# The end of an attention block on Trainium2: last logits on VectorE, last x on ScalarE, and the order of the work around them

## The chip, the cores and the metric

The kernel runs on one core of one Trainium2 chip. The metric is the time of one execution in microseconds (us), taken on the device. The core has five engines that run beside each other and meet at semaphores: TensorE (PE in the profile; PEld is its weight load), VectorE (DVE), ScalarE (ACT), GpSimd (POOL) and SyncE (SP), which here only issues DMA transfers. GpSimd issues DMAs too, among them the gathers and scatters by index.

## The reference

An attention block without softmax is followed by a mixture of experts with one expert per token:

```python
kv  = einsum('bhsd,bhse->bhde', k, v)            # batch 8, 8 heads, 576 tokens, head size 64
out = einsum('bhsd,bhde->bhse', q, kv)
out = out / sqrt(mean(out * out, -1) + 1e-6) * g_norm
x   = out.transpose(0, 2, 1, 3).reshape(4608, 512)

do     = x @ w_skip > 0                          # other tokens leave as they are
logits = x[do] @ w_gate                          # 8 experts
e      = argmax(logits);  p = softmax(logits)[e]
y      = relu(x[do] @ w1[e]) @ w2[e]             # 512 -> 1024 -> 512
result[do] = x[do] + p * y
```

All data are fp32.

## The kernel before

**Attention.** The kernel works through 36 units, `n` = 0 to 35; two neighbouring units (`u` = 0 and 1, four heads each) make 256 tokens' x. In step `n` of the main loop several units are in flight at once: `turn(n+1)` transposes q, `root(n-1)` (L525, ScalarE) takes the square root of the mean of squares, `values(n)` multiplies q with the state (L496, or L504 for units 34 and 35, which hold the ninth token of each group of nine) into a PSUM tile and squares it on ScalarE (L510), `squares(n)` sums the squares on VectorE (L518), and `norm(n-1)` takes the reciprocal (L532) and multiplies the PSUM tile by it (L537, `xl`). The state's columns hold, beside the 64 values of a head, 9 columns at each end with which the logits of the gate and the skip score come out of the same product. So an `xl` has both x and the parts of the logits. `finish(n-1)` adds the parts up on GpSimd (L554 for each unit, L558 and L562 for each pair, into `lg`), and puts the product of x with g_norm (L567, GpSimd, 128x512) on the list `late`. `scale` empties this list: for a unit it is called in the next unit's `norm`, where it waits for the reciprocal; the products of units 33 to 35 are emptied at step 36 behind the last instruction of the choice (L634). After a pair's second product, its x is stored to DRAM, by SP (L602, L591) or by GpSimd (L598).

PSUM tiles set part of the order: `o_ps` has two buffers, and units 30 and 33 use `sum_ps` in their place. A unit's L496 or L504 can start when the `xl` of the unit two before it (three for unit 33: unit 30) has read the tile.

**Queues.** The order of the instructions on each engine is that of the program, written by hand: `at(step, part, job)` puts a job into one of the parts of a step ("early", before `values`; "mid", after it; "pe", after `norm`; "dve"; "end"). No planner moves them.

**The choice and the slots.** Tiles of 128 tokens are gated in three groups, of 12, 10 and 14 tiles. `choose` (L614 to L634, VectorE) finds each token's expert, `rank` (L645 to L651, TensorE) counts places with triangular and full matrices of ones, `number` (L662 to L677, VectorE) splits each place into a column and a one-hot row (`oha_k`), `hits` (L690) and `weighed` (L698) make the columns, and `settle` (matmuls L710, sums L773) puts the token's row number into its slot. `NE` = 22 tiles are known before the last group. From the known ones `early` places the first 192 rows of the most frequent expert (`put`, L869 to L873, then `gather` L859 to L863, and `put_more`, L879, for the last 64 of them), `first_in` (L801, copies L828 and L830) turns these rows, and `first_layer_1` (L814, ReLU L817) starts the expert's first layer with them.

**The experts.** For the first expert `layer_1` (matmuls L1112, ReLU L1114 on ScalarE) and `layer_2` (L1124) work on the first 192 rows, f being the block of 128 of the 1024 hidden columns. Between these, TensorE takes up the rank and the slots of the last group, `again_rows` (L1051) copies indices of partial pieces between partitions, GpSimd gathers the remaining rows (L1084), and `expert_in` (L1093) turns them. Later experts follow one after another, with sums in the place of some products (L1192); each result is scattered by GpSimd (L1339). PSUM banks of the experts are the memory that the attention's tiles had: the third bank taken is the one of `first_layer_1`.

## Time and profile before

| | |
|---|---|
| median of 3 runs | 380.12 us (378.6 to 380.73) |
| the profiled execution | 381.81 us |
| its span | 380.0 us |
| TensorE busy in the span | 365.3 us (96%) |
| VectorE, ScalarE, GpSimd busy | 245.1, 142.3, 124.2 us |
| granted TensorE clock | 0.999 of full |

A span is the time from the first to the last instruction of one profiled execution. In a line of the timeline stand the start (us), the time of the whole run of equal instructions (us), engine, line of the program, operation, output and inputs, shapes and count; in brackets the idle time of the engine just before, and what ended it. A matrix product of fp32 shows as two records.

### The profile page before, as it was taken

To read this page: it belongs to the slowest core of one execution; us is meant where nothing else is said; L and a number is where in the kernel's file an instruction comes from. 1 tells how busy PE (TensorE), PEld (TensorE's weight loads), DVE (VectorE), ACT (ScalarE), POOL (GpSimd) and SP (SyncE) were. 2 spreads that over 40 slices of the span, in tenths; PEclk is the share of its full clock that TensorE was granted. 3 is DMA by queue.
4 is the path that set the end of the run, shared out by engine and by line. 5 is a ranking of instruction groups with operands and counts; after the bars stand their busy time and mean duration, and the time that the engine had idled before them with its cause. 6 is when DMAs were issued, how large, how long until landed. Compare 5 with 4: busy or idle time off the path is not lost.

```text
span 380.0 us, 9623 instructions
## 1 busy us (share of the span) xinstructions
PE 365.3 (96%) x3848; PEld 313.2 (82%) x3848; DVE 245.1 (64%) x626; ACT 142.3 (37%) x383; POOL 124.2 (33%) x195
## 2 busy tenths in 40 slices
PE   8999999999988998999999999999999999999994
PEld 4688797898977857779869987988988998998983
DVE  3344458667787961666756665875876876877831
ACT  2366676676774301214402430430440430431410
POOL 7025467655668544223013302212201211202003
PEclk9999999999999999999999999999999999999999
DMA  8999999996487738966516462672662762800001
GB/s 292 393 390 389 403 402 398 403 352 205 136 296 207 216 92 281 394 203 237 194 62 201 144 223 57 232 257 68 239 213 87 261 194 92 273 3 28 29 1 52
DMA packets 32039, 81.70 MB, mean 215 GB/s; under 512 B 2474, under 2 KB 2482, under 8 KB 31988
## 3 DMA queue, kind: packets, MB, share of 16 engines
q1 hardware_dynamic: 28176, 69.47, 52.1%
q0 software_dynamic: 3792, 11.53, 8.9%
q8 instruction: 32, 0.52, 0.6%
q14 instruction: 19, 0.16, 0.1%
q10 hardware_dynamic: 20, 0.02, 0.0%
HBM read 66.80 MB, written 14.48 MB: 214 GB/s over the span
## 4 chain that ended last, share of the span: by engine, by line
PE 84%; issue 6%; DVE 3%; ACT 3%; POOL 2%; DMA 1%; POOLq 0%; DVEq 0%; ACTq 0%
PE bank L1192 44%; PE bank L1124 9%; PE o_ps L496 6%; PE sum_ps L379 5%; PE bank L1112 4%; PE q_ps L460 3%; PE g_ps L393 2%; PE q_ps L170 2%; PE bank L1093 2%; DMA xg<-out_dram,src 1%; DVE rs L518 1%; DVE xl L537 1%; ACT sq L510 1%; PE q_ps L814 1%; PE g_ps L411 1%
## 5 line engine op out<-in xcount | busy, mean ns | idle before, releaser
L1202 ACT COPY p<-bank 128x128 f32<-128x128 f32 (+6 forms) x70 | 20.8, 297 | 100.3 <-PE bank L1192 89.3
L1192 PE MATMUL bank<-xt,w 128*128 128x128 f32 (+5 forms) x336 | 55.5, 288 | 0.1
L567 POOL TENSOR_TENSOR xb<-xl,g_b 128x512 f32<-128x512 f32 x36 | 44.4, 1234 | 32.5 <-DVE rs L532 30.6
L1192 PEld LDWEIGHTS bank<-xt,w 128*128 128x128 f32 x336 | 47.0, 190 | 2.0 <-DVE bank L1196 1.5
L1196 DVE TENSOR_TENSOR bank<-bank,p 128x128 f32<-128x128 f32 (+6 forms) x70 | 23.6, 337 | 37.1 <-PE bank L1192 36.0
L1192 PE MATMUL bank<-xs,s 128*128 128x128 f32 (+5 forms) x224 | 36.7, 289 | 0.0
L496 PE MATMUL o_ps<-kvd,qT 128*128 128x146 f32 x240 | 35.8, 290 | 1.0 <-ACT kvd L415 0.7
L1339 POOL DMA_INDIRECT out_dram<-xg,arows x9 | 10.0, 1112 | 78.7 <-DVE xg L1336 77.8
L518 DVE TENSOR_REDUCE rs<-sq 128x8 f32<-128x512 f32 x36 | 24.6, 682 | 16.2 <-ACT sq L510 16.0
L1124 PE MATMUL bank<-w,ht 128*32 128x128 f32 (+2 forms) x436 | 34.5, 319 | 0.0
L496 PEld LDWEIGHTS o_ps<-kvd,qT 128*128 128x128 f32 x240 | 31.6, 188 | 2.0 <-ACT kvd L415 1.5
L1192 PEld LDWEIGHTS bank<-xs,s 128*128 128x128 f32 x224 | 31.1, 190 | 1.0 <-ACT p L1202 0.8
L1339 POOL DMA_INDIRECT out_dram<-xg,rows x14 | 13.9, 994 | 53.2 <-DVE xg L1336 42.7
L1124 PEld LDWEIGHTS bank<-w,ht 128*32 128x32 f32 (+2 forms) x436 | 18.8, 120 | 13.2 <-issue 10.9
L537 DVE TENSOR_TENSOR xl<-o_ps,rs 128x584 f32<-128x584 f32 x34 | 26.1, 767 | 4.5 <-DVE rs L532 0.5
L1192 PE MATMUL bank<-t,ht 128*128 128x256 f32 x112 | 27.1, 385 | 0.0
L1192 PE MATMUL bank<-w,ht 128*128 128x256 f32 x112 | 27.1, 384 | 0.0
L1084 POOL DMA_INDIRECT xg<-out_dram,src x14 | 14.4, 1026 | 37.2 <-DMA out_dram<-xg,rows 13.9
L379 PE MATMUL sum_ps<-v,k 64*64 64x64 f32 x1152 | 25.6, 228 | 0.6 <-issue 0.6
L510 ACT ACTIVATE sq<-o_ps 128x512 f32<-128x512 f32 x34 | 20.3, 596 | 15.0 <-PE o_ps L496 14.5
L379 PEld LDWEIGHTS sum_ps<-v,k 64*64 64x64 f32 x1152 | 21.7, 140 | 4.7 <-issue 2.1
L1192 PE MATMUL bank<-t,hs 128*128 128x256 f32 x112 | 25.3, 379 | 0.0
(217 smaller groups left out, 680.5 us busy)
## 6 DMA issues: line engine op xcount, KB each, us to landing
w<-in_moe_w_dram SPq DMA_DIRECT2D x16, 2048.0 KB, 7.9
k<-in_k_dram SPq DMA_DIRECT2D x16, 576.0 KB, 9.7
v<-in_v_dram SPq DMA_DIRECT2D x16, 576.0 KB, 12.0
q<-in_q_dram SPq DMA_DIRECT2D x16, 576.0 KB, 9.2
out_dram<-xb SPq DMA_DIRECT2D x29, 256.0 KB, 4.4
out_dram<-xb POOLq DMA_DIRECT2D x7, 256.0 KB, 5.5
xg<-out_dram,src POOLq DMA_INDIRECT x16, 3.5
out_dram<-xg,rows POOLq DMA_INDIRECT x16, 7.1
```

The lines of the kernel that those rows point to most:

```text
L379: nc.tensor.matmul(out=sum_ps[w * 64:(w + 1) * 64, a, u, :], lhsT=kt[r, 2 * u + w, c, :], rhs=vt[r, 2 * u + w, c, :], start=(c == 0), stop ...
L496: nc.tensor.matmul(out=ps[:, w, 0:2 * PK].rearrange("p (r k) -> p r k", r=2)[:, :, cols], lhsT=qT[:, w, a, :], rhs=kvds[b % KVD][:, u, w, ...
L510: nc.scalar.activation(out=sq[:, :, :, :], in_=heads(ps, G, G + 2 * D), func=ACT.Square)
L518: nc.vector.tensor_reduce(out=rs[:, :, :], in_=sq[:, :, :, :].rearrange("p x y (a d) -> p x (y a) d", a=2), axis=AX.X, op=ALU.add)
L537: nc.vector.tensor_tensor(out=xl[:, :, :, :].rearrange("p x y (a k) -> p x (y a) k", a=2), in0=ps[:, :, 0:2 * PK].rearrange("p x (h k) -> ...
L567: late.append((lambda: nc.gpsimd.tensor_tensor(out=xb[:, :, 4 * u * D:(4 * u + 4) * D].rearrange("p r (w x) -> p r w x", w=2), in0=xl[:, : ...
L1112: nc.tensor.matmul(out=hps[:, cols], lhsT=w_sb[r][0][:, dc, f * P:(f + 1) * P], rhs=xt[:, dc, cols], start=(dc == 0), stop=(dc == DC - 1))
L1124: nc.tensor.matmul(out=yps[q * m:(q + 1) * m, 0:n], lhsT=ht(f)[:, off:off + m], rhs=w_sb[r][1][:, f, q * n:(q + 1) * n], start=(f == 0), s ...
L1192: nc.tensor.matmul(out=out, lhsT=lhsT(i), rhs=rhs(i), start=start and i == 0, stop=i == k - 1, skip_group_check=True)
L1196: nc.vector.tensor_tensor(out=to, in0=x, in1=y, op=ALU.add)
L1202: nc.scalar.copy(out=t, in_=x)
L1339: ins = nc.gpsimd.indirect_dma_start(out=cut_rows(m)[:, :], out_offset=bass.IndirectOffsetOnAxis(ap=rows[:, col:col + 1], axis=0), in_=x, ...
```

## The change

- `last_logits`: for units 34 and 35 no `xl` is made on VectorE. Two instructions for each unit multiply only the logits' parts by the reciprocal, from PSUM, and one reduction adds them up into `lgs`, all on VectorE. GpSimd's sums of these units are gone.
- `norm_by_scalar`: the x of these units is made by eight ScalarE instructions each (one for each of two rows or halves and four heads, 64 columns), queued after the last `root`; the products with g_norm follow as before, behind the choice, three in all with unit 33's.
- The ReLU of `first_layer_1` (L817) is queued after these, in the part "dve" of step 36.
- `put` empties `late` before its matmuls (unit 28's product, on GpSimd, with no wait for VectorE), makes the `hits` of the known tiles between its matmuls and L873, and calls `put_more` at once.
- `first_in(0)` moves behind `values(33)`.
- The order of TensorE's work from the rank to the first expert's remaining rows is another: one block f ahead of the rank (before: three), one before the known slots, three before the last slots (before: three, then `layer_2` of two f), then the last block, and all of `layer_2` after the slots.
- In the first expert two pieces of the next expert's rows are turned ahead of the gates' `again_of`, not one.

```diff
--- before.py
+++ after.py
@@ -534,16 +534,53 @@
             scale(n, inverse)
         r4 = rs[:, :, :].unsqueeze(3)
         xl = att_pool.tile([P, 2, 2, PK], FP32, tag="xl", name="xl", bufs=4)
+        if n >= NU - 2:
+            last_logits(n, ps, rs)
+            last_x.append(lambda: norm_by_scalar(n, ps, rs, xl))
+            return None
         nc.vector.tensor_tensor(
             out=xl[:, :, :, :].rearrange("p x y (a k) -> p x (y a) k", a=2),
             in0=ps[:, :, 0:2 * PK].rearrange("p x (h k) -> p x h k", k=KD),
             in1=r4.to_broadcast([P, 2, 4, KD]), op=ALU.mult)
         return lambda: finish(n, xl)
 
+    last_x = []
+
+    def place_of_logits(nq):
+        g = sum(2 * nq >= x for x in ends)
+        return g, 2 * nq - ([0] + ends)[g]
+
+    def last_logits(n, ps, rs):
+
+        nq, b, i, u = units[n]
+        assert i is None
+        if u == 0:
+            halves[nq] = att_pool.tile([P, 2, G, 8], FP32, tag="le", name="le", bufs=1)
+        le = halves[nq]
+        for a in range(2):
+            nc.vector.tensor_tensor(
+                out=le[:, :, :, 4 * u + a:4 * u + a + 3:2].rearrange("p r g w -> p r w g"),
+                in0=ends_of(heads(ps, 0, PK))[:, :, :, a, :],
+                in1=rs[:, :, a:a + 3:2].unsqueeze(3).to_broadcast([P, 2, 2, G]), op=ALU.mult)
+        if u == 1:
+            g, t0 = place_of_logits(nq)
+            nc.vector.tensor_reduce(out=lgs[g][:, t0:t0 + 2, :], in_=halves.pop(nq)[:, :, :, :],
+                                    axis=AX.X, op=ALU.add)
+
+    def norm_by_scalar(n, ps, rs, xl):
+
+        for r in range(2):
+            for h in range(4):
+                w, a = divmod(h, 2)
+                cols = slice(G + a * D, G + (a + 1) * D)
+                nc.scalar.activation(out=xl[:, r, w, cols],
+                                     in_=heads(ps, cols.start, cols.stop)[:, r, w, :],
+                                     func=ACT.Copy, scale=rs[:, r, h:h + 1])
+        weigh(n, xl)
+
     def finish(n, xl):
         nq, b, i, u = units[n]
-        g = sum(2 * nq >= x for x in ends)
-        t0 = 2 * nq - ([0] + ends)[g]
+        g, t0 = place_of_logits(nq)
         if t0 == 0 and u == 0:
             lgs[g] = gat_pool.tile([P, TG, G], FP32, tag="lg", name="lg", bufs=2)
         if u == 0:
@@ -561,6 +598,11 @@
                 lp[:, 0, :, :, :].rearrange("p r w g -> p w r g")
             nc.gpsimd.tensor_tensor(out=lgs[g][:, t0:t0 + 2, :], in0=both[:, 0, :, :],
                                     in1=both[:, 1, :, :], op=ALU.add)
+        weigh(n, xl)
+
+    def weigh(n, xl):
+
+        nq, b, i, u = units[n]
         if u == 0:
             xbs[nq] = xb_pool.tile([P, 2, DM], FP32, tag="xb", name="xb")
         xb = xbs[nq]
@@ -814,7 +856,7 @@
                 nc.tensor.matmul(out=hps[:, cols], lhsT=w_sb[0][0][:, dc, f * P:(f + 1) * P],
                                  rhs=xt_first[:, dc, :], start=(dc == 0), stop=(dc == DC - 1),
                                  skip_group_check=True)
-        at(NU, "early", lambda: nc.scalar.activation(
+        at(NU, "dve", lambda: nc.scalar.activation(
             out=ht_first[:, :, :], in_=hps[:, 0:IN * KEPT].rearrange("p (f t) -> p f t", f=IN),
             func=ACT.Relu))
 
@@ -838,6 +880,7 @@
     KNOWN = (ends[LAST - 1] - 2) // 4 * S
     assert ends[LAST - 1] == 4 * (KNOWN // S) + 2
     NE = ends[LAST - 1]
+    known_at = []
 
     def early():
 
@@ -865,10 +908,12 @@
                 in_offset=bass.IndirectOffsetOnAxis(ap=src[:, 0:1], axis=0))
 
         def put():
+            scale(now[0])
             for t in range(NE):
                 nc.tensor.matmul(out=ps, lhsT=oha_k[:, t, :],
                                  rhs=bv[:, t, :, :].rearrange("p c i -> p (c i)"), start=(t == 0),
                                  stop=(t == NE - 1), skip_group_check=True)
+            known_at.append(hits(0, NE, colid_i, gat_pool, NE))
             rows = gat_pool.tile([P, 2], FP32, tag="rows1", name="rows1")
             nc.vector.tensor_reduce(out=rows[:, :], in_=ps.rearrange("p (c i) -> p c i", i=2),
                                     axis=AX.X, op=ALU.add)
@@ -879,7 +924,7 @@
                 nc.tensor.matmul(out=more, lhsT=again[0, 64][:, :], rhs=rows[:, 1:2], start=True,
                                  stop=True, skip_group_check=True)
                 gather(more, 64, P)
-            at(now[0], "pe", put_more)
+            put_more()
         yield "mid", put
 
     load_kv(1)
@@ -944,7 +989,7 @@
     streams = []
     now = [0]
     for part in range(2):
-        at(NU - 3 + 2 * part, "early", lambda part=part: first_in(part))
+        at(*((NU - 3, "pe"), (NU - 1, "early"))[part], lambda part=part: first_in(part))
     at(NU - 1, "end", first_layer_1)
 
     PACE = (2, 4)
@@ -967,10 +1012,11 @@
         if done:
             done()
         if n == NU:
-            ohc = hits(0, NE, colid_i, gat_pool, NE)
+            for job in last_x:
+                job()
             drain(choose(LAST))
             scale(NU, chosen[-1])
-            first_bv = weighed(ohc, 0, NE, row_k, 2, gat_pool, NE)
+            first_bv = weighed(known_at[0], 0, NE, row_k, 2, gat_pool, NE)
         jobs(n, "dve")
 
         if n in ends[:LAST]:
@@ -1407,12 +1453,12 @@
                         result(first[0], yps0[0], xgs[0], tables, group)
                     else:
                         layer_1(r, xt, ht, slice(0, end), range(FC))
-                    enter(more[0:1])
+                    enter(more[0:2])
                     if yps0 is not None:
                         tables = again_gates(tables)
                         result(first[1], yps0[1], xgs[0], tables, group)
                     do(w1_sums(r + 1))
-                    enter(more[1:])
+                    enter(more[2:])
                 else:
                     fast_1(r, xt, ht, end // 2, w2_sums(r), lambda: enter(more[0:1]))
                     enter(more[1:])
@@ -1482,29 +1528,28 @@
         def ht_of(f):
             return ht_first[:, f, :] if f < IN else ht0[:, f, :]
 
-        layer_1(0, xt_first, ht0, slice(0, KEPT), range(IN, 5))
+        layer_1(0, xt_first, ht0, slice(0, KEPT), range(IN, 3))
         rank(LAST)
         drain(number(LAST))
-        layer_1(0, xt_first, ht0, slice(0, KEPT), range(5, FC))
+        layer_1(0, xt_first, ht0, slice(0, KEPT), range(3, 4))
         settle(0, NE, first_bv)
         last_bv = columns(NE, NT - NE, colid_i, row_k, 2, gat_pool, NE)
-        y, y_more = [layer_2(0, ht_of, piece, None, range(IN)) for piece in first]
+        layer_1(0, xt_first, ht0, slice(0, KEPT), range(4, 7))
         settle(NE, NT, last_bv)
-        layer_2(0, ht_of, first[0], y, range(IN, 3))
+        layer_1(0, xt_first, ht0, slice(0, KEPT), range(7, FC))
         arows = slot_pool.tile([P, NRES], I32, tag="arows", name="arows")
         asrc = slot_pool.tile([P, NRES], I32, tag="asrc", name="asrc")
         again_rows(arows, asrc, range(0, SOON))
         rows, src = slot_rows(slice(0, NCOL), slot_pool, "")
-        layer_2(0, ht_of, first[0], y, range(3, 4))
+        y, y_more = [layer_2(0, ht_of, piece, None, range(IN)) for piece in first]
         again_rows(arows, asrc, range(SOON, len(runs)))
-        layer_2(0, ht_of, first[0], y, range(4, FC))
         for r in range(3):
             gather_all(r, plan, src, asrc)
+        layer_2(0, ht_of, first[0], y, range(IN, FC))
         gates()
-        layer_2(0, ht_of, first[1], y_more, range(IN, 5))
         for piece in plan[0]:
             landed = expert_in(xg0, xt0, piece)
-        yps0 = [y, layer_2(0, ht_of, first[1], y_more, range(5, FC))]
+        yps0 = [y, layer_2(0, ht_of, first[1], y_more, range(IN, FC))]
         load_ahead(0, landed)
 
         def first_tables(layer, tables):
```

## The prediction

> **What bounds the kernel now.** I read the page first, then TensorE's timeline between 100 and 162 us (the stretch that the edits touch), then VectorE's, GpSimd's and ScalarE's timelines of the same stretch, to see what ends each of TensorE's gaps.
>
> ```profile
> span 380.0 us, 9623 instructions
> PE 365.3 (96%) x3848; PEld 313.2 (82%) x3848; DVE 245.1 (64%) x626; ACT 142.3 (37%) x383; POOL 124.2 (33%) x195
> ```
>
> TensorE is busy 365.3 of 380.0 us. By the stretches, it has 0.14 us of idle time between 160 and 360 us, so what is lost or won by 160 us is lost or won at the end. The edits add and take away no matmul; they can move the time only through TensorE's gaps. All gaps over 0.12 us between 100 and 162 us (start us, us, line, form, count, in brackets the idle time before and what ended it):
>
> ```profile
> 108.50 0.38 PE L879 MATMUL g_ps<-rows,again 128*128 128x1 f32 x2 [0.33 <-DVE rows L873]
> 113.27 0.63 PE L801 MATMUL q_ps<-ident,xg 128*128 128x128 f32 x4 [1.23 <-DMA xg<-out_dram,src]
> 117.38 0.74 PE L504 MATMUL o_ps<-kvd,q 64*64 64x73 f32 x32 [1.44 <-DVE xl L537]
> 118.56 2.87 PE L814 MATMUL q_ps<-xt_first,w 128*128 128x192 f32 x16 [0.44 <-ACT xt_first L830]
> 144.58 4.29 PE L1112 MATMUL bank<-xt,w 128*128 128x148 f32 x32 [0.60 <-issue]
> 149.46 0.73 PE L710 MATMUL g_ps<-bv,oha_k 128*128 128x72 bf16 x17 [0.49 <-issue]
> 155.58 0.28 PE L1051 MATMUL g_ps<-gate,ident 128*64 128x1 f32 x4 [0.24 <-DVE gate L773]
> ```
>
> They sum to 4.77 us, 1.25% of the span: the most that the change can win. From 118.56 to 143.98 TensorE never stops, so the choice (L614 to L634), the ranks and the slots are hidden there now. How well, VectorE and GpSimd show:
>
> ```profile
> 110.63 0.86 DVE L861 SCALAR_TENSOR_TENSOR src<-row 128x1 int32<-128x1 f32 x1
> 112.30 0.77 DVE L537 TENSOR_TENSOR xl<-sum_ps,rs 128x584 f32<-128x584 f32 x1
> 121.66 0.70 DVE L690 TENSOR_TENSOR ohc<-colid_i,hi_k 128x528 bf16<-128x528 int32 x1
> 123.14 0.27 DVE L614 TENSOR_REDUCE mx<-lg 128x14 f32<-128x112 f32 x1 [0.78 <-POOL lg L562]
> 124.77 1.25 DVE L698 TENSOR_TENSOR bv<-ohc,row_k 128x1056 bf16<-128x1056 bf16 x1
> 127.13 4.02 DVE L677 TENSOR_TENSOR oha_k<-row_i,lo_i 128x896 bf16<-128x896 int32 x2
> 131.91 0.86 DVE L698 TENSOR_TENSOR bv<-ohc,row_k 128x672 bf16<-128x672 bf16 x1
> ```
> ```profile
> 106.99 0.26 POOL L554 TENSOR_TENSOR lp<-xl 128x36 f32<-128x36 f32 x1
> 110.27 1.19 POOL L567 TENSOR_TENSOR xb<-xl,g_b 128x512 f32<-128x512 f32 x1
> 122.89 0.22 POOL L562 TENSOR_TENSOR lg<-lp 128x18 f32<-128x18 f32 x1
> 124.93 5.27 POOL L567 TENSOR_TENSOR xb<-xl,g_b 128x512 f32<-128x512 f32 x3 [1.82 <-DVE ohb L634]
> ```
>
> To see: the choice starts when GpSimd has made the last logits (123.11) and its last result is ready at 124.86. The slot columns of the last group are ready when L698 ends, 132.77; TensorE asks for them at 133.33, so 0.56 us of cover is left. And an L861 of one element took 0.86 us at 110.63 (0.16 at 108.73): it ended when GpSimd's product did, 111.46.
>
> **The skill.** "SBUF — State Buffer", section Who interferes with whom: a VectorE instruction with two inputs in SBUF and a GpSimd instruction that reads SBUF exclude each other for a whole instruction. The trace agrees: the L861 above; the three products of 1.18 us take 5.27; the two L677 take 2.0 each although a 256-column one takes 0.42, which makes some 1.0 for 896. L537 reads PSUM and takes 0.77 with or without a product beside it. "ScalarE: Activation LUTs", section What ACT_TABLE_LOAD costs: an ACTIVATE takes 186 ns + 0.833 ns a column, 93 more for each per-partition operand, and neighbours overlap by 93. The trace's 128x8 root with a bias operand took 0.30 (0.29 by that rule). It has no copy of 64 columns with a per-partition scale.
>
> **The change part by part**, in order of time; the units are numbered 0 to 35.
>
> 1. Slot placement in step 30 (`put`). The `hits` (L690, 0.70) move from 121.66 to between `put`'s matmuls and L873, where VectorE idles from 107.43 to 108.28: 0.85 us, so alone they cost nothing. But `scale` now puts unit 28's product (1.18) on GpSimd ahead of the gather, with no wait for VectorE: it follows the small sum at 106.99 and can start by 107.25. Both want the port. L850 holds it until 107.43; the product was there first, so it runs to 108.5, and the `hits` to 109.2. L873 starts at 109.2, not 108.28: +0.92 on the first gather and on L879, behind which TensorE's whole queue stands. Bounds: 0 if the `hits` get the port first, +1.1 if L850 loses it too. I take 0.92.
>  The other way, L859 and L861 of the second piece now follow at once, with the port free: 0.16 for 0.86, and the second gather is issued by 111.4, not 111.76.
> 2. The first rows' transposes (L801) behind `values(33)`: the 1.23 us wait for the gather goes, but `values(33)` writes sum_ps and cannot begin before unit 30's xl (112.30) has read it. That xl is late by the 0.92 of step 1, less 0.08 that VectorE wins back: 113.14, end 113.91. `values(33)` begins its load at 114.03, and before it did so at 113.62: **+0.4**. Its square, squares(33), xl(32), values(35), squares(34), root(34), and the copy L830 follow each other as now, so L814 starts at 118.96. Without the port's 0.92 the xl ends at 112.99 and the same chain gives 117.85, **-0.71**. The transposes then stand at 115.2, the rows landed by 114.1.
> 3. The last logits. Let T be L814's start. Now: T+6.30 for the choice's end (124.86-118.56). After: square of unit 35 ends at T+0.45 (119.01), squares to T+1.17, root to 1.50, reciprocal to 1.89 (0.19, behind unit 34's two logits of 0.2, at L845's 0.197 for 44 columns), two logits 2.0 to 2.35, their reduction (0.27) to 2.7, L614 at 2.73, end 1.72 later: **T+4.45**. GpSimd's own last sum, unit 33's, is done at 121.0, 0.7 before it is wanted. Won: 1.85, made of xl against logits (0.57 twice) and three GpSimd sums with their waits.
> 4. x on ScalarE: 16 ACTIVATEs of 64 columns, by the skill's rule 332 ns each less 93 of overlap, an estimate of 3.9 us in all, from T+1.5 to T+5.4, then L817 (0.49; moved behind them) to T+5.9. TensorE needs L817 for the bank of f=4 at T+6.85: hidden, with 0.95 to spare. Uncovered from 0.30 us each upward. GpSimd's product of unit 33 is waiting for the port until T+5.6, so units 34 and 35 come in time for their turns (T+6.7, T+8.9).
> 5. The new order of TensorE's work after L814 (2.71): f=2 (1.30), rank, f=3 (1.30), the known slots (0.55), f=4 to 6 (3.90), last slots. Rank waits for T+4.45 (0.28 idle) and ends at T+5.0, so the last slots are reached at T+10.75. Their columns come from a chain that is not changed: L698 until 1.17 after the choice (T+5.62), then 6.71 (126.06 to 132.77, port stalls included): T+12.4. TensorE waits **1.70**, with the rank's 0.28 **1.98**. Now it has 7.45 of work there (125.88 to 133.33), afterwards 5.75; the layer_2 work that was the cover is moved behind it. The gathers start some 2.7 us earlier against T, but their landing was not waited for (141.12 against 141.78).
> 6. Later: `expert_in` has 24 records of first[1] behind it, not 12, so the 0.60 before 144.58 (it ended with ScalarE's copy, 144.53) is covered: **-0.60**. Two pieces entered before the gates' L1051: **-0.24**. The 0.49 at 149.46 has no releaser in the profile; I count half, **-0.25**.
> 7. Queues: SP's load of the first expert's second matrix follows the moved transposes (115.64 to about 115.9); its packets end at 126 and layer_2 comes after 133. The last stores follow GpSimd's last product (now 130.2, then about 128.9) and land some 4 us later, 132.9, before the first gather's 134.2.
>
> Sum: +0.40 +1.98 -0.60 -0.24 -0.25 = +1.29 us. Against the span 380.0 that is 381.3; the profiled execution itself took 381.81, the median of the runs is 380.12, and I add the difference to the median: **381.4**.
>
> **Rivals.**
> - *The port costs nothing in step 30.* For it: L850 and the product ask within 0.2 us of each other. Against it: at 128.17 a waiting product got the port between two L677 of one queue. Then step 2 is -0.71: +0.18, 380.3.
> - *The gaps go and none is opened.* Needs, beside that, L677 free of the products, 2.2 us less in step 5's chain, more than its 1.70; 0.28 at the rank stays. That is so if unit 34's x comes after T+6.7, 0.65 us an activation; the trace's forms speak for 0.25. -0.71 +0.28 -0.60 -0.24 -0.49 = -1.76, and -2.04 with rank in time: 378.1.
> - *Slower: ScalarE's sixteen.* The bank of f=4 stays with L817. The first 0.95 us are spare and the next 1.70 lie in the wait for the slots, so it decides from (3.9+2.65)/16 = 0.41 us each; at 0.50 it adds 1.45: 382.9. Against it: 0.30 for the root.
>
> **How the numbers follow.** A measurement of this kernel can tell about 0.5%, 1.9 us, from no change. Main case 0.46 (own range 380.5 to 382.7; 0.16 beyond the bound); the first rival 0.22, within it; the second 0.22, of which 0.20 faster by over 0.5%; the third 0.10, slower. So faster 0.20, same 0.54, slower 0.26. The range, 378.2 to 383.0, reaches to the second and third rival's sums.
>
> **What would show it.** Right: L567 and L690 beside each other at 107 to 109 and L873 near 109.2; no wait for the gather before L801; L614 some 2.7 us after L814; a TensorE gap of 1 to 2 us ended by VectorE before the second slots' L710; no gap behind L1093. Wrong: L873 still at 108.3 (first rival); the two L677 at 1 us each (second); a gap before an L1112 ended by L817 or a ScalarE copy of 64 columns (third). A gap of TensorE beyond 160 us would break the frame of the argument.

## The result, and the profile after

The changed kernel takes 381.69 us (median of 11 runs, 380.57 to 383.13), the kernel before 380.11 (11 runs). The ratio is 1.0044, 95% interval 1.0029 to 1.0059: 1.1 to 2.2 us slower, a small loss, but one whose interval leaves out zero. In a second set of runs it was 1.0043 (1.0022 to 1.0065).

The page of the changed kernel: TensorE is again busy 96% of the span, so the question is again which of its gaps went and which came.

```profile
span 379.8 us, 9643 instructions
PE 364.8 (96%) x3848; PEld 314.2 (83%) x3848; DVE 245.1 (65%) x629; ACT 145.8 (38%) x399; POOL 123.0 (32%) x191
```

TensorE's timeline of the changed kernel, 100 to 162 us, gaps over 0.12 us (columns as before; L924, L843, L856, L752, L1158, L1139 and L1097 are the L879, L801, L814, L710, L1112, L1093 and L1051 of the kernel before, and on VectorE L732, L918 and L740 its L690, L873 and L698):

```profile
107.38 0.38 PE L924 MATMUL g_ps<-rows,again 128*128 128x1 f32 x2 [0.99 <-DVE rows L918]
113.56 1.24 PE L496 MATMUL sum_ps<-kvd,qT 128*128 128x146 f32 x8 [0.97 <-DVE xl L541]
117.27 0.74 PE L504 MATMUL o_ps<-kvd,q 64*64 64x73 f32 x32 [0.81 <-DVE xl L541]
118.46 2.87 PE L856 MATMUL q_ps<-xt_first,w 128*128 128x192 f32 x16 [0.44 <-ACT xt_first L872]
130.79 0.51 PE L752 MATMUL g_ps<-bv,oha_k 128*128 128x48 bf16 x14 [1.33 <-DVE bv L740]
145.29 4.29 PE L1158 MATMUL bank<-xt,w 128*128 128x148 f32 x32
```

The wait of 1.23 for the gather is gone, and in its place stands one of 0.97 for the xl of unit 30. The one in front of the last unit is 0.81 instead of 1.44. The gap in front of `put_more` has tripled, 0.33 to 0.99. A new one, 1.33, ends with VectorE's columns for the last slots. No gap stands before L1158, and none at 149 or at the gates' copies. From 107.7 to 111.1 us this execution ran at half the TensorE clock (last section), so the times up to T below are longer than those of an undisturbed one.

VectorE's timeline of the changed kernel, in `put` and from the last logits to the last slots, and then GpSimd's of the same places:

```profile
105.56 1.69 DVE L732 TENSOR_TENSOR ohc<-colid_i,hi_k 128x528 bf16<-128x528 int32 x1
107.18 0.15 DVE L918 TENSOR_REDUCE rows<-g_ps 128x2 f32<-128x4 f32 x1
121.11 0.27 DVE L656 TENSOR_REDUCE mx<-lg 128x14 f32<-128x112 f32 x1
122.55 0.28 DVE L676 TENSOR_TENSOR ohb<-eorder,fi 128x112 bf16<-128x112 f32 x1
129.88 0.86 DVE L740 TENSOR_TENSOR bv<-ohc,row_k 128x672 bf16<-128x672 bf16 x1
```
```profile
105.43 1.26 POOL L609 TENSOR_TENSOR xb<-xl,g_b 128x512 f32<-128x512 f32 x1
122.90 5.27 POOL L609 TENSOR_TENSOR xb<-xl,g_b 128x512 f32<-128x512 f32 x3 [2.58 <-DVE ohb L676]
136.84 1.05 POOL L1130 DMA_INDIRECT xg<-out_dram,asrc  x1 [8.54 <-PE g_ps L1097]
```

The `hits` (L732) took 1.69 us beside a GpSimd product of 1.26. With T the start of the first layer (L856, 118.46), the choice begins at T+2.65 and ends at T+4.37. The columns are there at T+12.3, and TensorE, which by the profile had come to them at T+11.0, waits. ScalarE's sixteen (L576) and the ReLU behind them, on its timeline:

```profile
120.26 3.38 ACT L576 ACTIVATE xl<-o_ps,rs 128x64 f32<-128x64 f32 x16 [0.30 <-DVE rs L532]
123.41 0.61 ACT L859 ACTIVATE xg<-q_ps 128x384 f32<-128x384 f32 x1
```

They are over at T+5.6, before TensorE wants the bank: no gap is ended by ScalarE after T.

### The profile page after: what moved, and what is told of

Same layout as the page of the kernel before. It is cut to its first block, busy times and chain, and to the rows that moved or that the text cites. A ratio compares the mean times of both kernels' runs of the same rounds, so it can differ in the third digit from the quotient of the medians.

```text
span 379.8 us, 9643 instructions
## 1 busy us (share of the span) xinstructions
PE 364.8 (96%) x3848; PEld 314.2 (83%) x3848; DVE 245.1 (65%) x629; ACT 145.8 (38%) x399; POOL 123.0 (32%) x191
## 4 chain that ended last, share of the span: by engine, by line
PE 80%; issue 6%; DVE 6%; DMA 3%; ACT 2%; POOL 1%; POOLq 0%; DVEq 0%; ACTq 0%
PE bank L1238 44%; PE bank L1170 9%; PE o_ps L496 6%; PE sum_ps L379 4%; PE q_ps L460 3%; DMA q<-in_q_dram 3%; PE bank L1158 3%; PE g_ps L393 2%; PE bank L1139 2%; PE q_ps L170 2%; DVE oha_k L719 1%; DVE rs L518 1%; ACT sq L510 1%; DVE xl L541 1%; PE g_ps L1097 1%
## 5 line engine op out<-in xcount | busy, mean ns | idle before, releaser
L496 PE MATMUL o_ps<-kvd,qT 128*128 128x146 f32 x240 | 36.8, 296 | 1.0 <-ACT kvd L415 0.7
L496 PEld LDWEIGHTS o_ps<-kvd,qT 128*128 128x128 f32 x240 | 32.5, 193 | 2.0 <-ACT kvd L415 1.5
L1170 PEld LDWEIGHTS bank<-w,ht 128*32 128x32 f32 (+2 forms) x436 | 19.1, 120 | 13.6 <-issue 11.1
L541 DVE TENSOR_TENSOR xl<-o_ps,rs 128x584 f32<-128x584 f32 x32 | 24.5, 767 | 4.3 <-DVE rs L532 0.5
L379 PE MATMUL sum_ps<-v,k 64*64 64x64 f32 x1152 | 24.7, 223 | 0.5 <-issue 0.5
L379 PEld LDWEIGHTS sum_ps<-v,k 64*64 64x64 f32 x1152 | 20.8, 134 | 4.4 <-issue 2.0
```

The source lines that it names most:

```text
L379: nc.tensor.matmul(out=sum_ps[w * 64:(w + 1) * 64, a, u, :], lhsT=kt[r, 2 * u + w, c, :], rhs=vt[r, 2 * u + w, c, :], start=(c == 0), stop ...
L496: nc.tensor.matmul(out=ps[:, w, 0:2 * PK].rearrange("p (r k) -> p r k", r=2)[:, :, cols], lhsT=qT[:, w, a, :], rhs=kvds[b % KVD][:, u, w, ...
L541: nc.vector.tensor_tensor(out=xl[:, :, :, :].rearrange("p x y (a k) -> p x (y a) k", a=2), in0=ps[:, :, 0:2 * PK].rearrange("p x (h k) -> ...
L1170: nc.tensor.matmul(out=yps[q * m:(q + 1) * m, 0:n], lhsT=ht(f)[:, off:off + m], rhs=w_sb[r][1][:, f, q * n:(q + 1) * n], start=(f == 0), s ...
```

## The experiments

For each trace four times are read from TensorE's timeline: **a**, from the first product of `put`'s placement to T (L856, formerly L814); **b**, from T to the first expert's remaining rows (L1158, formerly L1112); **c**, from there to the last half of `layer_2` behind the gates; and the rest up to the last matmul, which lay between 216.95 and 217.49 in all of them. a is where the first two steps of the prediction act, b the third to fifth, c the sixth. What lies ahead of a took 105.70 to 107.85 us, with no order among the kernels, so single executions are not compared by their whole time. "Cover" is work that TensorE still has while another engine makes what it needs next.

### The kernel before, once more

> The kernel before once more, unchanged, for a second profile of it. The forecast credited the change with two idle times of the first profile behind the first layer's rows, 0.60 us at 143.99 and 0.49 us at 148.97. If they belong to the kernel, they stand in this profile too, 26.0 us from the first layer's start to the remaining rows' first product; if they belong to that one execution, at least one is missing, and that way is about 25.4 us, as in e6_logits_alone.

The profile of before had gaps of 0.60 at 143.99 and 0.49 at 148.97, both with no releaser, from which the prediction took credit. Before the first, ScalarE's copy of the rows began 1.2 us after the transposes' end. In a second profile of the same program neither is there (TensorE's timeline):

```profile
118.00 4.55 PE L814 MATMUL q_ps<-xt_first,w 128*128 128x192 f32 x16 [0.44 <-ACT xt_first L830]
145.03 4.29 PE L1112 MATMUL bank<-xt,w 128*128 128x148 f32 x32
155.30 0.28 PE L1051 MATMUL g_ps<-gate,ident 128*64 128x1 f32 x4 [0.23 <-DVE gate L773]
```

L1112 starts without a gap, and only the gates' 0.23 is left. Gaps of 0.4 to 0.7 turn up between 144 and 153 us in three of the other profiles below, and in the rest not, whatever the order of work. They belong to an execution, not to a program. L814 shows something else of this kind: 4.55 us for 2.87 before, at half the TensorE clock (last section). The run took 381.49 us, like the first profiled one (381.81), above the median of 380.11.

So the undisturbed kernel before has a = 11.0 to 11.1, b = 25.36 (from the next experiment, where TensorE's order of work behind T is the same) and c = 12.19. Of these a is the least firm: a later run with the same order up to T (TensorE's new order alone) has 10.78, because the gather was waited for 0.93 us and not 1.15 to 1.23.

### The last logits and ScalarE's x alone

```diff
 # the kernel before, and in norm():
+        if n >= NU - 2:
+            last_logits(n, ps, rs)
+            last_x.append(lambda: norm_by_scalar(n, ps, rs, xl))
+            return None
 # the ReLU of first_layer_1 in "dve" behind last_x; put, first_in and TensorE's order as before
```

> The kernel before with one part of the change alone: the last logits on VectorE, the last x on ScalarE, the first layer's ReLU behind it. My theory (the choice comes about 2 us earlier against the first layer's start, less the hits, which now stand in its way, but TensorE has its cover there anyway): the same time as before within 0.3 us, the choice's last instruction 5.0 to 5.2 us after the first layer's start, not 6.3, and no gap on TensorE made or closed. Rival (the earlier choice pays, through earlier gathers): 0.5 us or more faster. Rival (ScalarE's sixteen hold up a bank): slower with a gap before an L1112-like product that ScalarE ends.

Measured: 380.09 against 380.14 us, 1.0000 (0.9984 to 1.0017). a = 11.08, b = 25.36, c = 12.19. The choice ends at T+5.0 (ohb 122.36 + 0.28, T = 117.64), 1.3 us earlier than before, even with the `hits` still between logits and choice, and it is worth nothing: TensorE comes to the rank only at T+6.8.

```profile
117.64 2.87 PE L856 MATMUL q_ps<-xt_first,w 128*128 128x192 f32 x16 [0.44 <-ACT xt_first L872]
124.46 0.21 PE L690 MATMUL g_ps<-ohb,ut 128*128 128x112 bf16 x1
```

### TensorE's new order alone

```diff
-        layer_1(0, xt_first, ht0, slice(0, KEPT), range(IN, 5))
+        layer_1(0, xt_first, ht0, slice(0, KEPT), range(IN, 3))
         rank(LAST)
 ...
+        layer_1(0, xt_first, ht0, slice(0, KEPT), range(4, 7))
         settle(NE, NT, last_bv)
 # and the rest of that part of the diff; everything else as before
```

> The kernel before with the change's order of TensorE's work between the rank and the remaining rows alone; the last logits stay on GpSimd. My theory (the earlier choice of the change only pays for a part of the cover that its order takes away): the rank is reached 4.0 us after the first layer's start and waits until 6.3, the last slots wait 1.3 to 1.8 us more, so 3.5 to 3.9 us over the kernel before, ratio 1.009 to 1.010; and since the logits alone gave nothing, the two parts don't add up. Rival (the wait for the last slots belongs to the port and GpSimd's products, whatever the order): a single gap of about 1.3 us, ratio 1.004.

Measured: 382.47 against 380.09, 1.0076 (1.0048 to 1.0103), a little under what was expected. b = 28.82, 3.46 more than the order before. With the choice as late as before, TensorE waits for it and for the slots (timeline):

```profile
123.82 0.21 PE L648 MATMUL g_ps<-ohb,ut 128*128 128x112 bf16 x1 [2.03 <-DVE ohb L634]
131.73 0.51 PE L710 MATMUL g_ps<-bv,oha_k 128*128 128x48 bf16 x14 [1.32 <-DVE bv L698]
```

So the order takes away 3.4 us of cover, and the earlier choice gives back 2.0 of them (b falls to the changed kernel's 26.83), nearly all of the wait at the rank. The slots' wait is the same, 1.32 and 1.33: the rank releases VectorE's chain to the columns, which come 7.9 us after the start of L648 (L690 in the changed kernel), and TensorE is there 6.6 us after it, in both.

### The changes in `put` alone

```diff
         def put():
+            scale(now[0])
             for t in range(NE):
 ...
+            known_at.append(hits(0, NE, colid_i, gat_pool, NE))
             rows = gat_pool.tile([P, 2], FP32, tag="rows1", name="rows1")
 ...
-            at(now[0], "pe", put_more)
+            put_more()
```

> The kernel before with the change's edits of the slot placement alone: unit 28's product ahead of the gather, the hits behind the placement's matmuls, the second piece at once. My theory (the product and the hits exclude each other, and the first gather is late by that): hits of 1.6 to 1.7 us, L873 0.9 us later against the placement, the first layer's start 12.0 us after the placement and not 11.1, and 0.9 us over the kernel before: ratio 1.002 to 1.003. Rival (the slack of the gather's way swallows it): 11.1 us and the time of the kernel before.

Measured: 380.68 against 380.09, 1.0009 (0.9989 to 1.003). The collision is there as in the changed kernel (VectorE's, then TensorE's timeline):

```profile
106.06 1.69 DVE L690 TENSOR_TENSOR ohc<-colid_i,hi_k 128x528 bf16<-128x528 int32 x1
```
```profile
107.88 0.38 PE L882 MATMUL g_ps<-rows,again 128*128 128x1 f32 x2 [0.99 <-DVE rows L876]
112.11 0.63 PE L801 MATMUL q_ps<-ident,xg 128*128 128x128 f32 x4 [0.43 <-DMA xg<-out_dram,src]
```

But a is 11.21, not the 12.0 that was expected: that was a miss. `put_more` comes 0.67 later, and yet the transposes (L801) start only 0.13 to 0.44 later behind `put` than in the profiles of the old order. TensorE waits for the gather in both, so this was no slack: the first gather's rows were there 3.84 us after their indices, for 4.08 to 4.38 in those profiles. Why they came faster is not shown; the second piece's indices no longer stall (0.16 for 0.86), and its gather is issued at once.

### The first rows turned later, alone

```diff
-    for part in range(2):
-        at(NU - 3 + 2 * part, "early", lambda part=part: first_in(part))
+    for part in range(2):
+        at(*((NU - 3, "pe"), (NU - 1, "early"))[part], lambda part=part: first_in(part))
```

> The kernel before with one part of the change alone: the transposes of the first 128 rows behind unit 33's products. My theory: unit 33 now waits for unit 30's xl (end 113.07) and not for the gather (113.13, transposes until 113.73), so it starts 0.5 us earlier and the first layer's start with it: 379.5 to 379.8 us. Rival (the rows' copy then comes too late on ScalarE and the first layer waits for it): 380.1 or more.

Measured: 380.78 against 381.62, 0.997 (0.9956 to 0.9984); a = 10.63, 0.45 less. The gather's wait is replaced by the wait for the xl of unit 30, which is almost as long:

```profile
112.06 1.24 PE L496 MATMUL sum_ps<-kvd,qT 128*128 128x146 f32 x8 [1.17 <-DVE xl L537]
```

The part that pays is the next: 0.81 before the last unit, for 1.44.

### The changed kernel without the product in `put`

```diff
         def put():
-            scale(now[0])
             for t in range(NE):
```

> The changed kernel with unit 28's product left where it was, behind the next reciprocal, so that nothing of GpSimd's stands beside the moved hits; all other parts of the change stay. My theory (the two exclude each other at the port, and TensorE's queue stands behind L879 for it): the hits take 0.70 us and not 1.69, L873 follows the placement's matmuls, the gap before L879 falls from 0.99 to about 0.3, and the half clock that the changed kernel's trace shows from 107.7 to 111.1 us goes with the gap: 1.1 us for the delay and up to 0.6 more for the clock, so 379.8 to 380.6 us against 381.7. Rival (the delay is hidden behind the waits for xl that follow, and the clock falls for another reason): within 0.3 us of the changed kernel.

Measured: 381.47 against 381.62, 1.0007 (0.9988 to 1.0025). The `hits` take 0.70, `put_more`'s gap is 0.32 and a = 10.56. This shows that the product held up the `hits` and `put_more`. But b grew from 26.83 to 27.41: unit 28's product, no longer done early, pushes GpSimd's later sums back, the choice now waits for GpSimd, and the rank for the choice. So of the 1.1 us and more that were expected the traces' sum leaves 0.1, the medians at full clock 0.7. The run of both edits below has both readings.

### The cover given back

```diff
-        layer_1(0, xt_first, ht0, slice(0, KEPT), range(4, 7))
+        layer_1(0, xt_first, ht0, slice(0, KEPT), range(4, FC))
         settle(NE, NT, last_bv)
-        layer_1(0, xt_first, ht0, slice(0, KEPT), range(7, FC))
+        y = layer_2(0, ht_of, first[0], None, range(IN))
 ...
-        y, y_more = [layer_2(0, ht_of, piece, None, range(IN)) for piece in first]
+        y_more = layer_2(0, ht_of, first[1], None, range(IN))
```

> The changed kernel with more of TensorE's work ahead of the last slots: block f=7 of the first layer before them, and the second layer's first two blocks split around the two copies of indices. My theory (the last slots are reached before their columns are ready, because the cover was taken away): the gap of 1.33 us that a VectorE product ends is gone or under 0.1 us and does not come back elsewhere, so 1.2 to 1.4 us less than the changed kernel, 380.3 to 380.5. Rival (the later slots delay the gathers, and the rows' transposes wait for them): a new gap before L1139 of about the same size, no gain.

Measured: 381.68 against 381.62, 0.9988 (0.9972 to 1.0004). One more block before the last slots takes the gap of 1.33 away and b falls from 26.83 to 25.41; it doesn't come back later. One block of 1.3 us was missing (TensorE's timeline):

```profile
127.42 5.45 PE L1158 MATMUL bank<-xt_first,w 128*128 128x192 f32 x32
132.89 0.51 PE L752 MATMUL g_ps<-bv,oha_k 128*128 128x48 bf16 x14
```

Both edits together:

> Both of the edits of the two runs beside this one. If the two terms are apart in time and add up, 2.3 to 3.1 us less than the changed kernel: 378.6 to 379.4, which is 0.7 to 1.5 us under the kernel before, that is the rest of what the change was to win. If they are one and the same wait that only moves, about as the better of the two alone.

Measured: 380.02 against 381.62, 0.9965 (0.995 to 0.9981). VectorE's and TensorE's timelines of this kernel:

```profile
107.30 0.70 DVE L732 TENSOR_TENSOR ohc<-colid_i,hi_k 128x528 bf16<-128x528 int32 x1
121.21 0.27 DVE L656 TENSOR_REDUCE mx<-lg 128x14 f32<-128x112 f32 x1 [0.67 <-POOL lg L599]
```
```profile
122.98 0.21 PE L690 MATMUL g_ps<-ohb,ut 128*128 128x112 bf16 x1 [0.61 <-DVE ohb L676]
```

The port is free, the choice is 0.67 late for GpSimd's sum, and the rank waits 0.61. What is left is to cover the rank too.

### All of it covered

```diff
 # on top of both edits
-        layer_1(0, xt_first, ht0, slice(0, KEPT), range(IN, 3))
+        layer_1(0, xt_first, ht0, slice(0, KEPT), range(IN, 4))
         rank(LAST)
 ...
-        layer_1(0, xt_first, ht0, slice(0, KEPT), range(3, 4))
+        layer_1(0, xt_first, ht0, slice(0, KEPT), range(4, 5))
         settle(0, NE, first_bv)
 ...
+        layer_1(0, xt_first, ht0, slice(0, KEPT), range(5, FC))
+        y = layer_2(0, ht_of, first[0], None, range(IN))
         settle(NE, NT, last_bv)
+        y_more = layer_2(0, ht_of, first[1], None, range(IN))
 ...
 # between the two copies of indices, where layer_2's first blocks were:
+        layer_2(0, ht_of, first[0], y, range(IN, 3))
```

> e3_both with two more moves in TensorE's order: two blocks f ahead of the rank (the 0.61 us wait for the choice), and the second layer's first two blocks for the first 128 rows ahead of the last slots. If these waits are covered and come back nowhere else, 0.5 to 0.7 us less than e3_both: ratio to the kernel before 0.9945 to 0.9955, about 379.5 us. If another wait takes their place (the gathers, or the copies of indices right after the slots), the time of e3_both.

Measured: 378.40 against 380.14, 0.9954 (0.994 to 0.9967). This version beats both kernels, by 1.7 us the one before. TensorE's timeline has no gap from T to the end of the gates:

```profile
122.78 0.21 PE L690 MATMUL g_ps<-ohb,ut 128*128 128x112 bf16 x1
129.20 1.88 PE L1169 MATMUL bank<-w,xg 128*128 128x512 f32 x4
130.92 0.51 PE L752 MATMUL g_ps<-bv,oha_k 128*128 128x48 bf16 x14
```

a = 10.55, b = 24.71, c = 11.89. b is 0.65 shorter than in the kernel before although neither has an idle moment there. By the starts, the 48 records of `layer_2` up to L1157 take 10.7 us here and 11.4 where, as before, the two pieces' products of 512 and of 256 columns follow one another in a finer mix. That this mix is the cause was not tried.

### The gap in `put` filled

```diff
+            for _ in range(16):
+                nc.tensor.matmul(out=g_ps[:, GB + 8:GB + 8 + P], lhsT=ones[:, :], rhs=ones[:, :],
+                                 start=True, stop=True, skip_group_check=True)
             known_at.append(hits(0, NE, colid_i, gat_pool, NE))
```

Sixteen bf16 products whose results nothing uses stand in the 0.99 us gap; the rest is the changed kernel. The question was the clock: in both profiles of the changed kernel it halves for 3.4 us, from 0.3 and from about 1.5 us after this gap's end (last section).

> The changed kernel with 16 bf16 products of 128x128 added on TensorE behind the slot placement's, into an unused part of the bank, so that TensorE works through most of the gap of 0.99 us before L879's copy of indices; their results are not used. The delay of L873 by the port stays. My theory (the half clock of 3.4 us that follows this gap in the traces of the changed kernel and of e2_cover comes from TensorE's idleness there, and is a second price of the collision): no half clock after it, the way from the placement to the first layer's start falls from 12.7 to about 11.6 us, and the time by about 1 us. Rival (the half clock is set off by something else, or costs nothing behind the waits that follow): the same 12.7 us and the same time as the changed kernel, or longer by the products.

Measured: 381.65 against 380.14, 1.0038 (1.0022 to 1.0054), beside 381.75 for the changed kernel again on the same chip, for which the expectation was:

> The changed kernel once more, unchanged, beside the runs of the kernel before that the other experiments share. If the ratio of 1.0044 (1.0029 to 1.0059) holds beside those, 382.9 to 383.6 us where the kernel before has about 381.6; if it is lower here, the distances to the changed kernel are to be taken from this run.

The profile with the filling has no half clock after the gap's place. a is 11.47, against 12.76 and 12.19 with half clock, but the median is the same: the expected 1 us was a miss. Two things explain it by the numbers. The filling itself makes `put_more` later, since L921 reads the tile that the products write: 1.93 us after `put`'s first product, for 1.69 (timeline):

```profile
107.82 1.05 PE L917 MATMUL g_ps<-ones 128*128 128x128 bf16 x16
109.20 0.38 PE L927 MATMUL g_ps<-rows,again 128*128 128x1 f32 x2 [0.32 <-DVE rows L921]
```

And the clock falls in some executions only. Of the changed kernel's 23 runs 11 had a mean clock below 0.996 and 12 had not, so a median over them is near that of the undisturbed ones (381.5, against 382.5 to 382.7 for the others). The median hides what the filling did. On the chip that ran both, 5 of the changed kernel's 12 runs had a mean clock of 0.993 or lower; of the 15 filled runs none was below 0.995, the clock of the profiled one, whose only fall lies between 7 and 11 us. The longest filled run took 382.24 us, the longest of the changed kernel 383.19, and the mean is 381.44 for 381.82. This speaks for a fall that goes with the gap and costs some 0.4 us on average.

### The sum over all runs

From the traces, a + b + c against 11.08 + 25.36 + 12.19 of the kernel before; where half clock or a gap without a cause lies inside, the undisturbed value of the same order is put in (marked). Beside it the difference of the medians of all runs, and of those with a mean clock of at least 0.996:

| kernel | a | b | c | by the trace | medians | medians, full clock |
|---|---|---|---|---|---|---|
| logits alone | 11.08 | 25.36 | 12.19 | 0 | -0.05 | -0.3 |
| `put` alone | 11.21 | 25.36 | 12.19 | +0.1 | +0.6 | -0.7 |
| order alone | 10.78 | 28.82 | 12.19 | +3.2 | +2.4 | +2.8 |
| rows later | 10.63 | 25.36* | 12.19* | -0.45 | -0.8 | +0.2 |
| changed kernel | 11.23* | 26.83 | 11.89 | +1.3 | +1.6 | +1.8 |
| the same, filled | 11.47 | 26.82 | 11.89 | +1.55 | +1.5 | +1.8 |
| without the early product | 10.56 | 27.41 | 11.89* | +1.2 | -0.2 | +1.1 |
| cover given back | 11.23* | 25.41 | 11.89* | -0.1 | +0.1 | -0.1 |
| both | 10.55 | 25.99 | 11.89* | -0.2 | -1.6 | -0.4 |
| all covered | 10.55 | 24.71 | 11.89 | -1.5 | -1.7 | -1.8 |

The 11.23 is the a of "both", 10.55, and the 0.67 by which the collision delays `put_more` in the changed kernel (1.69 us behind `put`'s first product for 1.02); from there to T the four profiles of this order without half clock (filled, without the early product, both, all covered) have the same 9.54 us. In the last column each lies within 0.8 us of the trace's sum, so the table tells differences of 1 us and more, not those of 0.5: a alone changes by 0.3 from one execution of the same order to the next. The wide misses of the column "medians" (without the early product, both) come from one chip, where the kernel before had a low mean clock in 43 of 65 runs and a median of 381.62; in runs with a full clock they go.

## Why the prediction was right

381.4 was predicted and 381.69 measured, inside the main case's own range of 380.5 to 382.7. In short: the earlier choice was worth nothing where TensorE still had work, and the order that was to use it took more cover away than the choice gave back (+1.47 us between T and the remaining rows); the gates' gap went (-0.30), and T came 0.15 to 0.45 later. That is the mechanism forecast, but the sum held by luck in part, since two errors cancel.

**Step 1, the collision: right, over-sized.** The product got the port first, the `hits` behind it took 1.69, and the first gather's rows came late. L918 stands 1.48 us behind `put`'s first product for 0.80: +0.68, not +0.92, since the `hits` end 0.56 behind the product, not 0.70.

**Step 2, T +0.40: right in sign, its size open.** The changed kernel's undisturbed a is 11.23; the four profiles with the order of before up to T have 10.78, 11.00, 11.08 and 11.08. So T comes 0.15 to 0.45 later. Without the collision (10.55) it comes 0.23 to 0.53 earlier, for a forecast of 0.71. The exchange of the gather's wait for the xl of unit 30 is as forecast, and so is the shorter wait before the last unit.

**Step 3, the choice at T+4.45: right**, T+4.37, begun at T+2.65 for 2.73.

**Step 4, ScalarE's sixteen: right that they are hidden, over-sized.** "ScalarE: Activation LUTs", section What ACT_TABLE_LOAD costs, gave an estimate of 3.9 us; they took 3.38, 0.20 from start to start. The third rival, which needed 0.41 each, is excluded.

**Step 5, 1.98 of waits: right in place, over-sized.** The columns came when forecast (taken up at T+12.33, forecast 12.4; less 10.75 that is 1.65, not 1.70). The profile's idle time of 1.33 starts at the modelled end of the run before it. From start to start, the 24 products ahead of the last slots take 5.47 us for 3.98 where nothing is waited for: a wait of 1.49. The rank's product starts 0.42 behind L687, for 0.21 in the kernel before. Together 1.70. Beside the waits, TensorE's own work changed its length, which the forecast left out when it said that the edits can move the time only through TensorE's gaps: `layer_1` cut into four pieces needs 8.14 us from start to start, without the wait, for the 7.88 of two pieces (1.30, 1.38, 3.98 and 1.48, for 3.90 and 3.98), and `layer_2`, mixed less finely, 10.88 for 11.37. In all b grew by 1.47. That the wait would be one for slots and not for the choice is what the runs with the logits alone and with the order alone show.

**Step 6: one of three terms right.** The gates' gap went, -0.30 in c for -0.24. The -0.60 and the -0.25 failed: those gaps are not in the second profile of the kernel before, nor in those of the logits alone and of `put` alone, which have its order of work there, so the change could not remove them. What failed is the sum's base: credits were read from an execution of 381.81 us, and the result added to a median of 380.12 that need not hold those gaps. One may not do both. Without them the forecast would have been +2.14, 382.3, above the result; with what the traces show for T (+0.15 to +0.45), b (+1.47) and c (-0.30) it comes to +1.3 to +1.6.

**Step 7: wrong on the gathers.** Step 5 has them start 2.7 us earlier against T. They start at T+18.4, T+18.1 before. The profile puts the first one's wait down to TensorE (L1097, in the line of GpSimd above), but the second copy of indices is not what it needs: in the kernel before the same gather starts ahead of VectorE's first use of that copy.

```profile
136.70 1.05 POOL L1084 DMA_INDIRECT xg<-out_dram,asrc  x1 [6.37 <-DVE src L782]
136.90 0.22 DVE L1067 TENSOR_SCALAR arows<-g_ps,q_f 128x1 int32<-128x1 f32 x1 [0.43 <-PE g_ps L1051]
```

Its own index was there by 134.08 in the changed kernel. But it writes columns of `xg0` in which `ht_first` lies, and `layer_2`'s first twelve products read that until 136.06:

```profile
133.08 2.98 PE L1170 MATMUL bank<-w,xg 128*128 128x512 f32 x12
```

In the changed kernel these twelve stand behind the last slots, in the kernel before ahead of them. In all the profiles in which they stand there (the changed kernel twice, filled, order alone, without the early product, cover given back, both; in the last two eight of the twelve) the gather starts 0.78 or 0.79 us after their end. No run was made to part this from L1097, which follows the twelve; the kernel's text and these starts agree. The prediction followed the slots and forgot the memory that the gather writes. It cost nothing: the transposes (L1139) follow at 141.91 with no gap.

**The rivals.** The first (no cost at the port, 380.3) needed L873 at its old place: excluded. The second (378.1) needed L677 free of the products; in the changed kernel L719 still took 4.02 for the two. With the logits alone, where GpSimd's products were over at 127.15 and the first L719 began at 126.06, the two took 3.04: the second ran without a product beside it, in about 1.0, as that rival has it. That a version without gaps behind T exists is shown by the one with all covered, 378.40.

**What stays open.** The full-clock medians put the changed kernel at +1.8 us, the trace's sum at +1.3, or +1.6 with the smallest a of the old order; the interval, 1.1 to 2.2, holds all of them. Part of the difference may lie behind c, which the sum leaves out: 216.95 to 217.18 us in the profiles of the kernel before and of single parts of the change, and 217.18 to 217.49 in those of the changed kernel and its variants. Why was not looked for.

## What to carry to other kernels

Moving a producer earlier is worth only what its consumer was waiting, and reordering the consumer to use it uncovers every later hand-over of the same chain: here the choice was 1.9 us earlier, but rank, slot columns and second slots follow one another with some 8 us of VectorE's work between rank and columns, and what was put behind the rank must be as long as that. A gap that the profile gives no releaser should be looked for in a second profile before it is counted as a gain. And a work put into the idle 0.85 us of one engine may be held up by one that another engine has at the same time: the `hits` of 0.70 took 1.69 beside GpSimd's product of 1.26, and 0.70 with the product elsewhere, where it cost 0.58 at the choice instead.

## What the runs showed of the hardware

**TensorE's clock was halved after short gaps, in some executions.** Windows of the changed kernel's first profile (start and end, length, busy time and count for each of PE, PEld, DVE, ACT and POOL, then the granted clock, the DMA share and GB/s):

```profile
104.30:107.70 3.40, 2.36 (x37) 2.08 (x35) 3.33 (x7) 2.06 (x6) 2.39 (x3) 1.00 1.01 377
107.70:111.10 3.40, 3.40 (x17) 3.39 (x17) 1.92 (x6) 0.78 (x2) 2.58 (x4) 0.50 0.76 270
```

For 3.4 us the clock is 0.50, and a unit's eight products took 2.15 us for 1.17. "TensorE: Matmul & The Clock Gate", section What's actually happening, gives half clock after at least one idle window of about 3.4 us. Here TensorE had been busy 2.36 of the 3.4 us ahead, with no single gap above 0.99; in the kernel before's second profile it was busy 1.53 of 3.4, with no gap above 1.43, and L814 took 4.55 for 2.87. The measurement decides: stretches busy by 45 to 69% were followed by half clock. Other executions kept the full clock there: `put` alone with the same gap and the same 2.36 of 3.4, the first profile of before and the logits alone with 1.58 and 1.57 of 3.4 ahead of T. So such gaps make the fall possible, not certain. The filled kernel, with a mean clock of at least 0.995 in all of its 15 runs, speaks for the gap as a cause; what else decides was not found.

**A fall costs less than it shows.** It lengthened L814 by 1.7 us where TensorE was the bound, and a by 1.0 and 1.5 in the two profiles of the changed kernel (12.19 and 12.76 for 11.23). A mean clock below 0.996 stands for a fall anywhere: of the 13 profiles the eight below it have one, and the five above have none. Five of the eight have one of some 3.4 us between 7 and 11 us, where no version differs, two of them beside the later one. Runs below 0.996 are some 1 us longer than the others of their kernel (380.8 and 379.7 for the kernel before, 382.5 and 381.5 for the changed one), on one chip 1.8 (382.1 and 380.3, before). The changed kernel has them in 11 of 23 runs, the kernel before in 12 of 27, 33 of 55 and 43 of 65 by chip, so they do not explain the difference between the two, which is 1.8 us without them too.
